# A second layer by Strassen's scheme one pass earlier, with its output weights stored and half of them combined in the first pass

## The chip, the core and the metric

One core of a Trainium2 chip runs the whole kernel. The metric is device time in microseconds (us), from one launch of the program; the time before is the median of three runs. Engines are called by their trace names: PE is TensorE (matmuls; PEld its weight loads), DVE is VectorE, ACT is ScalarE, POOL is GpSimd, SP is SyncE, which here issues all DMA transfers.

## The reference

Decayed linear attention without a softmax, for 8 batches of 8 heads, 576 positions and head size 64, and behind it a feed-forward layer on 4,608 tokens (512 to 2,048 to 512):

```python
scores = scale * np.matmul(q, k.transpose(0, 1, 3, 2))
Dmat = np.where(rel >= 0, gamma[:, None, None] ** rel[None, :, :], 0.0)
attn = np.matmul(scores * Dmat[None, :, :, :], v)
x = attn.transpose(0, 2, 1, 3).reshape(B * S, H * D)
h = x @ w_in
g = np.maximum(h, 0.0) + np.log1p(np.exp(-np.abs(h)))     # softplus
return g @ w_out
```

## The kernel before

Every float32 operand of a matmul is split into a high and a low part of the faster format float32r, and each product is made of three matmuls (low x high, high x low, high x high). All large matmuls are 128 x 128 by 512 columns.

The tokens are nine units of 512. Unit 0 is computed while the weights arrive. The other eight go in four passes of two units: pass 0 has units 1 and 2, pass 1 units 3 and 4, and so on. In a pass the first layer is done by Strassen's scheme on 2 x 2 blocks (seven products in place of eight), over the two units, two halves of the input and a pair of 128-wide pieces of the hidden layer. There are eight such pairs, J = 0 to 7 in the code (NJ = 8). A product takes six matmuls (`product`, line 876 in its loop).

The second layer has two forms:

- Plain: for each piece p of the hidden layer and each 128 tokens, three matmuls into one of four banks y (`output_mm`, line 510). The softplus values of the second unit are sent to DRAM as kept parts and fetched again when that unit's turn comes.
- Full: the softplus values of both units stay on chip in G (the tiles g, placed over the output weights' own tiles, which by then have been stored to DRAM), and the second layer too is done with seven block products (`second`, line 1164). Its weight blocks come from DRAM through the ring: plain ones from outsplit, combined ones (sums S1 to S4 of blocks) from outcombined. Two of the seven are done inside a pair (`full_pair`); five follow as phases over all eight pairs (`full_phase`), the first of which, S4, collects in the PSUM tile named two.

`FULL = 2` says that passes 0 and 1 use the plain form and passes 2 and 3 the full form.

Pass 0 is mixed in its first layer too. While the combined input weights are not all there, pairs 0 to 4 of units 1 and 2 run as ten plain slots each (`plain_slot`: two products, twelve matmuls of the second layer, and in every other slot one attention group). Between those of unit 1 and those of unit 2 the Strassen pairs 5 to 7 run (`strassen_pair`). Then unit 2 finishes from its kept parts. By the trace, unit 1's slots start at about 118 us, pass 1 at 315.15, pass 2 at 500.57 and pass 3 at 676.41.

Attention goes on beside all this: 29 groups of small 64 x 64 matmuls (`chunk_products`), one each in two slots or one pair, each for a chunk of 128 tokens. It computes the scores of one chunk and the values of the one before, into two and third; DVE then masks the scores out of two (L252, tile a), scales the values out of two (L437, tile xs) and updates the states from third (L279, L290). The operands keys and qv are loaded one group ahead, and POOL scales the part v of qv (L187) before the sums of that group use it.

Every engine works through its instructions in the order in which the code issues them. Weight blocks go through a ring of eight tiles; each `product` or `second` requests the block for the eighth one behind it. Combining an output pair j is three steps: `whole_out` (DVE, two sums of high and low, L657), `combine_out` (DVE, four operations on 128x256, L670), and the split into high and low (ACT L674, two casts; DVE L678, two differences), and then two stores of 512 KB to outcombined. Storing it plainly (`store_plain`) is a store of 256 KB and one of 512 KB to outsplit. Before the change this is done in pass 1, pair by pair, and for pair 7 partly in pass 2. In unit 1's slots and the Strassen pairs of pass 0 the input weights are combined by the same operations (`prepare...`), and the combinations of x for the next pass are made by `start...` and `finish...`.

## Time and profile before

| | us |
|---|---|
| median of 3 runs | 830.55 |
| the three runs | 829.44, 830.55, 835.12 |
| the profiled execution, its own time | 834.61 |
| its span from the first to the last instruction | 832.8 |
| PE busy | 822.0 (99%) |
| DVE busy | 516.3 (62%) |
| ACT busy | 377.2 (45%) |
| DMA packets of the data queue | 204.26 MB, 73.7% of 16 engines |

Matmuls overlap, so PE's busy time shows that it is hardly ever without one and not how long a single one takes; for that, a chain of equal matmuls is divided by their number. The views used are the page, the chain in order of time, the waits, the timelines of single engines and the busy time by stretch.

### The profile page before, as it was taken

Reading aid. Unit: us, or ns where it says so; the run is one execution under the profiler, and the core shown is the slowest. Engines: PE = TensorE matmul, PEld = TensorE weight load, DVE = VectorE, ACT = ScalarE, POOL = GpSimd, SP = SyncE. Lnnn points to the kernel's source line nnn. Section 1 sums busy time; section 2 is a strip of 40 time slices with the busy share of each in tenths; the row PEclk is TensorE's granted clock in tenths of the full one; section 3 lists DMA queues with packets and bytes.
Section 4 is the critical chain, followed back from the end, with each engine's and each line's share of the span. In section 5 each row is a group of like instructions: output and inputs, shape, how many; then the busy total and the mean of one; then the engine's idle time right before and its main releaser. Section 6 shows DMA issues by size and latency. Waiting matters only on the chain.

```text
span 832.8 us, 18575 instructions
## 1 busy us (share of the span) xinstructions
PE 822.0 (99%) x7367; PEld 676.3 (81%) x7367; DVE 516.3 (62%) x883; ACT 377.2 (45%) x655; POOL 119.3 (14%) x223
## 2 busy tenths in 40 slices
PE   8999999999999999998999999999999999999998
PEld 6788888888888888887888888888888888888886
DVE  5998967664456686554553753564768953234786
ACT  6888863244332245332432443433345644344553
POOL 4312321221221410111111000211100000000000
PEclk9999999999999999999999999999999999999999
DMA  9998879767778754997989516878856686666674
GB/s 358 313 312 302 297 249 388 247 221 247 252 232 288 250 201 132 352 325 257 311 302 316 195 51 220 273 250 271 277 157 218 197 261 197 193 193 194 196 217 158
DMA packets 138069, 205.44 MB, mean 247 GB/s; under 512 B 10368, under 2 KB 99968, under 8 KB 137984
## 3 DMA queue, kind: packets, MB, share of 16 engines
q1 hardware_dynamic: 137984, 204.26, 73.7%
q8 instruction: 59, 0.97, 0.5%
q14 instruction: 26, 0.21, 0.1%
HBM read 157.56 MB, written 46.66 MB: 245 GB/s over the span
## 4 chain that ended last, share of the span: by engine, by line
PE 94%; DMA 3%; DVE 2%; issue 0%; SPq 0%; ACT 0%; DVEq 0%
PE y L510 27%; PE acc L876 21%; PE two L876 13%; PE sum L1164 12%; PE h L476 5%; PE third L876 3%; PE two L1164 3%; PE third L210 2%; PE two L194 2%; PE two L298 2%; PE two L310 1%; DMA raw<-others 1%; PE third L1164 1%; PE acc L1164 1%; DMA raw<-whole 1%
## 5 line engine op out<-in xcount | busy, mean ns | idle before, releaser
L510 PE MATMUL y<-wout,g 128*128 128x512 f32 x960 | 234.6, 393 | 0.7 <-DVE g L498 0.7
L510 PEld LDWEIGHTS y<-wout,g 128*128 128x128 f32 x960 | 179.3, 189 | 38.9 <-PE h L476 1.1
L876 PE MATMUL acc<-xt,ring 128*128 128x512 f32 x780 | 196.7, 390 | 0.0
L876 PEld LDWEIGHTS acc<-xt,ring 128*128 128x128 f32 x780 | 146.8, 188 | 30.9
L876 PE MATMUL two<-xt,ring 128*128 128x512 f32 x486 | 123.6, 390 | 0.0
L1164 PE MATMUL sum<-parts,ring 128*128 128x512 f32 (+1 forms) x483 | 115.7, 390 | 0.1
L876 PEld LDWEIGHTS two<-xt,ring 128*128 128x128 f32 x486 | 91.1, 188 | 19.4 <-DVE g L1189 0.5
L1164 PEld LDWEIGHTS sum<-parts,ring 128*128 128x128 f32 x483 | 89.7, 188 | 19.2 <-DVE parts L1157 0.5
L1157 DVE TENSOR_TENSOR parts<-g,parts 128x512 fp32r<-128x512 f32 x112 | 75.5, 687 | 40.3 <-ACT parts L1153 37.6
L1153 ACT CAST parts<-g 128x512 fp32r<-128x512 f32 x112 | 69.3, 623 | 47.5 <-PE sum L1164 18.1
L494 ACT CAST g<-ab 128x512 fp32r<-128x512 f32 x58 | 36.0, 621 | 72.5 <-PE y L510 66.9
L187 POOL TENSOR_TENSOR qv<-qv,consts_sb 128x256 f32<-128x256 f32 x61 | 44.6, 732 | 164.4 <-DMA qv<-others 156.8
L498 DVE TENSOR_TENSOR g<-ab,g 128x512 fp32r<-128x512 f32 x58 | 42.6, 735 | 27.1 <-ACT g L494 26.5
L1174 ACT ACTIVATE g<-g 128x512 f32<-128x512 f32 x48 | 30.2, 629 | 42.4 <-DVE g L1189 24.8
L1189 DVE TENSOR_TENSOR g<-two,g 128x512 f32<-128x512 f32 x16 | 11.1, 691 | 61.8 <-PE two L876 59.1
L476 PE MATMUL h<-xt,win 128*128 128x512 f32 x192 | 47.5, 396 | 0.0
L252 DVE TENSOR_TENSOR a<-two,mask 128x512 f32<-128x512 f32 (+1 forms) x28 | 19.0, 678 | 44.5 <-PE third L210 24.7
L476 PEld LDWEIGHTS h<-xt,win 128*128 128x128 f32 x192 | 35.3, 188 | 8.1 <-DVE win L596 0.5
L502 ACT ACTIVATE ab<-quad 128x512 f32<-128x512 f32 x33 | 20.9, 632 | 38.7 <-DVE quad L1008 16.1
L210 PEld LDWEIGHTS third<-qv,keys 64*64 64x64 f32 x776 | 27.1, 134 | 8.9 <-issue 8.1
L210 PE MATMUL third<-qv,keys 64*64 64x64 f32 x776 | 32.8, 222 | 0.1
L194 PE MATMUL two<-qv,keys 64*64 64x64 f32 x880 | 31.5, 221 | 0.0
(173 smaller groups left out, 1123.3 us busy)
## 6 DMA issues: line engine op xcount, KB each, us to landing
ring<-split SPq DMA_DIRECT2D x121, 256.0 KB, 4.2
ring<-combined SPq DMA_DIRECT2D x108, 256.0 KB, 3.9
qv<-others SPq DMA_DIRECT2D x61, 320.0 KB, 5.0
wst<-w SPq DMA_DIRECT2D x32, 512.0 KB, 6.2
ring<-outcombined SPq DMA_DIRECT2D x64, 256.0 KB, 3.4
keys<-others SPq DMA_DIRECT2D x61, 256.0 KB, 5.1
ring<-outsplit SPq DMA_DIRECT2D x48, 256.0 KB, 3.4
split<-win SPq DMA_DIRECT2D x16, 512.0 KB, 6.6
```

What stands on the lines that cost most here:

```text
L187: nc.gpsimd.tensor_mul(v, v, f.unsqueeze(2).broadcast_to([P, 4, D]))
L194: nc.tensor.matmul(L["S"][rows[t], h, part[s]], L["k"][rows[h], s, part[t]], L["q"][rows[h], s, part[t]], start=True, stop=True, skip_grou ...
L210: mm = nc.tensor.matmul(L["T"][rows[h], t, part[s]], L["kp"][rows[t], s, rows[h]], L["v"][rows[t], s, rows[h]], start=True, stop=True, ski ...
L476: nc.tensor.matmul(h, wins[p][:, a, kt * P:(kt + 1) * P], xt[:, b, T1 + half, kt % 2], start=(n == 0), stop=(n == 3 * NKT - 1))
L494: nc.scalar.copy(g[:, HI], ab)
L498: nc.vector.tensor_sub(g[:, LO], ab, g[:, HI].bitcast(F32))
L510: nc.tensor.matmul(ys[u][tt], g[:, a, tt * P:(tt + 1) * P], wouts[p][:, b], start=(p == 0 and n == 0), stop=(p == NF - 1 and n == 2))
L876: nc.tensor.matmul(bank, w[:, ta, kt * P:(kt + 1) * P], xt[:, tb, x, kt], start=start and k == 0, stop=k == 5, skip_group_check=True)
L1153: nc.scalar.copy(t[:, HI], g_slot(J, n))
L1157: nc.vector.tensor_sub(t[:, LO], g_slot(J, n), t[:, HI].bitcast(F32))
L1164: nc.tensor.matmul(bank[m][:, x], w[:, a, m * P:(m + 1) * P], t[:, b, x], start=start and n == 0, stop=n == 2, skip_group_check=True)
L1174: nc.scalar.activation(c, c, AF.Softplus)
```

## The change

`FULL` becomes 1: pass 1 too does its second layer in the full form. G lies over the tiles of the output weights, so these have to be stored before pass 1, and their combinations 4 to 7 have to be read from them before the pair that covers them.

- All eight plain stores move into pass 0: pairs 0 to 4 in unit 1's slots 1, 3, 5, 7, 9, pairs 5 to 7 in unit 2's slots 0, 2, 4 (they are queued and leave with the next products).
- Output pairs 0 to 3 are combined in pass 0: 0 in unit 1's slots 3 to 8, 1 and 2 in Strassen pairs 6 and 7, 3 in unit 2's slots 4 to 8. The preparation of input pairs 7 and 4 moves into Strassen pair 5.
- Output pairs 4 to 7 are combined inside the full pairs of pass 1; the job lists of pass 1 and pass 2 differ from before in that, and in where the combined x is started. The split of block B22 for pass 2 moves into its pair 0.

```diff
-FULL = 2
+FULL = 1
@@ unit 1's slots, (slot, function, arguments)
-        (2, prepare_store, PLAIN), (2, half_b22, 0), (2, start_here, 0), (2, prepare_whole, PLAIN + 1, 0, 1),
-        (3, finish_here, 0), (3, prepare_whole, PLAIN + 1, 1), (4, half_b22, 1), (4, start_here, 1),
...
+        (2, prepare_store, PLAIN), (2, half_b22, 0), (2, start_here, 0), (2, prepare_whole, PLAIN + 1),
+        (3, finish_here, 0), (3, whole_out, 0), (4, half_b22, 1), (4, start_here, 1), (4, prepare_sums, PLAIN + 1),
+        (5, finish_here, 1), (5, prepare_split, PLAIN + 1), (5, combine_out, 0, 0, 2), (5, prepare, PLAIN + 2),
+        (6, prepare_store, PLAIN + 1), (6, half_b22, 2), (6, start_here, 2), (6, combine_out, 0, 2),
+        (7, finish_here, 2), (7, split_out, 0), (7, prepare_ring, PLAIN - 1, 0, 2), (8, store_out, 0),
+        (8, half_b22, 3), (8, start_here, 3), (8, prepare_ring, PLAIN - 1, 2, 4), (9, finish_here, 3),
+        (9, prepare_whole, PLAIN + 2), *[(2 * j + 1, store_plain, j) for j in range(PLAIN)])
@@ Strassen pairs
-    extras = {(FULL - 1, J): J for J in range(NJ - 1)}
-    earlier = {(0, PLAIN): (PLAIN + 2,), (0, PLAIN + 1): (PLAIN - 1,)}
+    extras = {(0, PLAIN + 1): 1, (0, PLAIN + 2): 2}
+    earlier = {(0, PLAIN): (PLAIN + 2, PLAIN - 1)}
@@ unit 2's slots
+            more_jobs = schedule((4, whole_out, 3), (6, combine_out, 3), (7, split_out, 3), (8, store_out, 3),
+                                 *[(2 * n, store_plain, first + n) for n in range(NJ - first)])
@@ full passes
         if s == FULL:
-            last = NJ - 1
-            job(0, lambda: whole_out(last, spare[:2]))
-            job(1, combine_out, last)
-            job(2, lambda: combine_split(raws["out", last]))
-            job(3, queue_store, last)
+            for at, f, *args in ((0, whole_there, 4, 0), (0, whole_there, 5, 2), (1, combine_out, 4), (2, split_out, 4),
+                                 (2, queue_store, 4), (2, combine_out, 5), (3, split_out, 5), (3, queue_store, 5),
+                                 (3, whole_there, 6, 0), (4, combine_out, 6), (4, whole_there, 7, 2),
+                                 (5, split_out, 6), (5, queue_store, 6), (5, combine_out, 7), (6, split_out, 7),
+                                 (6, queue_store, 7), (6, start, 0)):
+                job(at, f, *args)
         if more:
-            for i in range(2):
-                job(4 + i, start, i)
+            if s == FULL:
+                job(divmod(15, NJ), start, 1)
+            else:
+                for i in range(2):
+                    job(4 + i, start, i)
...
-        else:
+        if s > FULL:
             job("x", half_x, B22, STAGE[1, 1], whole, nc.vector)
```

A job with number n of a full pass runs in pair n + 1.

Three places show the order. The first is PE in a pair of pass 1 (attention left out): of before, pair 1 (the numbers behind y and wout are those of the tiles):

```order
L876 MATMUL acc<-xt,ring 128x512 x6
L876 MATMUL two<-xt,ring 128x512 x6
L510 MATMUL y_4274<-wout_179,g 128x512 x3
L510 MATMUL y_4275<-wout_179,g 128x512 x3
L876 MATMUL two<-xt,ring 128x512 x6
L876 MATMUL acc<-xt,ring 128x512 x6
L876 MATMUL two<-xt,ring 128x512 x6
L510 MATMUL y_4276<-wout_179,g 128x512 x3
L510 MATMUL y_4277<-wout_179,g 128x512 x3
L876 MATMUL acc<-xt,ring 128x512 x6
```

and of the change, the same pair (L1167 is what line 1164 was):

```order
L876 MATMUL acc<-xt,ring 128x512 x6
L876 MATMUL two<-xt,ring 128x512 x6
L876 MATMUL acc<-xt,ring 128x512 x6
L876 MATMUL two<-xt,ring 128x512 x6
L876 MATMUL acc<-xt,ring 128x512 x6
L876 MATMUL two<-xt,ring 128x512 x6
L1167 MATMUL sum<-parts,ring 128x512 x6
L876 MATMUL acc<-xt,ring 128x512 x6
L1167 MATMUL sum<-parts,ring 128x512 x6
```

The rows of line 510 are gone from the pair, and two blocks of the full form have come; its other five follow behind pair 7. Over a pass that is 384 matmuls of line 510 against 336.

The second place is DVE at the end of pair 7, the last before the phases. Before (pass 2, which is the first full pass; L1157 splits one G tile into the parts of a second-layer block):

```order
L1251 TENSOR_TENSOR g_7055<-g_7055 128x512
L1252 TENSOR_TENSOR g_7055<-g_7055,g_7054 128x512
L1157 TENSOR_TENSOR parts<-g_5952,parts 128x512
L437 TENSOR_TENSOR xs<-two,consts_sb 128x2x2x128
L1157 TENSOR_TENSOR parts<-g_6164,parts 128x512
```

and of the change (pass 1, now the first full pass; L1254, L1255 and L1160 are the lines that were L1251, L1252 and L1157):

```order
L1254 TENSOR_TENSOR g_5212<-g_5212 128x512
L1255 TENSOR_TENSOR g_5212<-g_5212,g_5211 128x512
L678 TENSOR_TENSOR quad<-quad 128x512 x2
L456 TENSOR_TENSOR quad<-xs 128x256
L457 TENSOR_TENSOR quad<-xs,quad 128x256
L458 TENSOR_TENSOR quad<-xs 128x256
L459 TENSOR_TENSOR quad<-xs,quad 128x256
L1160 TENSOR_TENSOR parts<-g_4110,parts 128x512
L252 TENSOR_TENSOR a<-two,mask 128x512
L437 TENSOR_TENSOR xs<-two,consts_sb 128x2x2x128
L279 TENSOR_TENSOR u<-third,s 128x256
L290 TENSOR_TENSOR s<-third,u 128x256
```

The split of output pair 7 and the start of a combined x now stand ahead of the read-outs of two (L252, L437), and there is a masked read-out, since pass 1's last group has scores.

The third place is SP in unit 1's slots 1 and 2, one piece of the difference (split is the input weights, outsplit the plain output weights):

```order
 L628 DMA ring<-split_112 128x2x256 x2
-L628 DMA ring<-split_113 128x2x256 x2
+L628 DMA ring<-split_113 128x2x256
+L980 DMA outsplit_139<-wout_179 256x1x256
+L628 DMA ring<-split_113 128x2x256
+L982 DMA outsplit_140<-wout_180 128x1024
 L146 DMA keys<-others 128x512
 L152 DMA qv<-others 128x640
```

Two stores of output pair 0 have come in ahead of the operands of an attention group; pairs 1 to 7 follow in the same way.

## Rows read from the trace of the kernel before

**Rows 1.** The page, parts 1 and 4: busy time, and the last chain by engine

```profile
PE 822.0 (99%) x7367; PEld 676.3 (81%) x7367; DVE 516.3 (62%) x883; ACT 377.2 (45%) x655; POOL 119.3 (14%) x223
PE 94%; DMA 3%; DVE 2%; issue 0%; SPq 0%; ACT 0%; DVEq 0%
```

**Rows 2.** Waits of PE: us in total, times, longest us

```profile
PE two L310 <- issue: 2.3, 1, 2.3
```

**Rows 3.** The chain in order of time: start us, us, what

```profile
144.87 2.72 PE acc L876 x12
...
238.61 2.72 PE acc L876 x12
...
347.98 1.59 PE y L510 x6
...
365.18 1.59 PE y L510 x6
...
382.27 2.31 issue
...
403.82 1.59 PE y L510 x6
...
508.91 5.44 PE y L510 x24
...
590.26 1.59 PE sum L1164 x6
...
620.28 9.52 PE two L1164 x42
```

**Rows 4.** The page, part 5: busy us and mean ns of line 510's matmuls

```profile
L510 PE MATMUL y<-wout,g 128*128 128x512 f32 x960 | 234.6, 393 | 0.7 <-DVE g L498 0.7
```

**Rows 5.** One stretch: length, busy us (instructions) by engine, PEclk, DMA share, GB/s

```profile
385.00:388.50 3.50, 3.50 (x10) 2.73 (x10) 2.04 (x4) 0.59 (x1) 1.40 (x3) 0.51 0.70 258
```

**Rows 6.** DMA from 382 to 383.2 us: packets, MB, share of 16 engines

```profile
q8 instruction: 1, 0.02, 4.6%
```

**Rows 7.** Passes 1 and 2, line 510 alone: length, PE, PEld, PEclk, DMA

```profile
315.15:500.57 185.42, 94.53 (x385) 72.18 (x384) 0.99 0.73 252
500.57:676.41 175.84, 5.60 (x24) 4.50 (x24) 1.00 0.74 236
```

**Rows 8.** Pass 2, line 1164 alone, same columns

```profile
500.57:676.41 175.84, 80.00 (x336) 62.36 (x336) 1.00 0.74 236
```

**Rows 9.** Timeline of DVE, pairs 3 and 5 of pass 2: start us, us, what

```profile
559.11 1.28 DVE L678 TENSOR_TENSOR quad<-quad 128x512 fp32r<-128x512 f32 x2
...
588.09 0.42 DVE L456 TENSOR_TENSOR quad<-xs 128x256 f32<-128x256 f32 x1
...
589.22 0.42 DVE L459 TENSOR_TENSOR quad<-xs,quad 128x256 f32<-128x256 f32 x1
590.31 0.69 DVE L252 TENSOR_TENSOR a<-two,mask 128x512 f32<-128x512 f32 x1 [0.67 <-PE third L210]
590.92 0.68 DVE L437 TENSOR_TENSOR xs<-two,consts_sb 128x512 f32<-128x512 f32 x1
```

**Rows 10.** Three stretches, columns as in rows 5

```profile
118.00:142.00 24.00, 23.93 (x245) 19.61 (x244) 14.62 (x28) 9.41 (x16) 5.54 (x12) 1.00 1.02 356
142.00:304.00 162.00, 162.00 (x1935) 134.34 (x1934) 97.16 (x177) 54.22 (x92) 39.40 (x69) 1.00 0.77 258
...
334.00:455.00 121.00, 118.69 (x1272) 98.12 (x1272) 59.72 (x105) 43.92 (x74) 16.74 (x35) 0.99 0.90 309
```

**Rows 11.** Timeline of POOL, the second scaling of v of a group

```profile
145.61 0.77 POOL L187 TENSOR_TENSOR qv<-qv,consts_sb 128x256 f32<-128x256 f32 x1 [0.85 <-DMA qv<-others]
...
238.05 0.62 POOL L187 TENSOR_TENSOR qv<-qv,consts_sb 128x256 f32<-128x256 f32 x1 [0.88 <-DMA qv<-others]
```

**Rows 12.** Timeline of SP, the stores of unit 2's slot 8

```profile
289.07 1.03 SPq L686 DMA_DIRECT2D combined<-quad  x2
```

**Rows 13.** Timeline of ACT, the first read of kept part 5

```profile
301.59 0.62 ACT L494 CAST g<-quad 128x512 fp32r<-128x512 f32 x1 [1.10 <-PE y L510]
```

More of the change, by code (lines that the diff above doesn't have):

```diff
@@ L657, in whole_out, with combine_out @@
             nc.vector.tensor_add(a[:, HI], w[:, HI].bitcast(F32), w[:, LO].bitcast(F32))
-    def combine_out(j):
+    def combine_out(j, first=0, upto=4):
         f = raws["out", j]
@@ L662, in combine_out @@
         (a11, a21), (a12, a22) = ((a[:, 0], a[:, 1]) for a in blocks[0])
-        combine_blocks(a11, a12, a21, a22, blocks[1], nc.vector)
+        combine_blocks(a11, a12, a21, a22, blocks[1], nc.vector, first, upto)
     def combine_blocks(a11, a12, a21, a22, sums, engine, first=0, upto=4):
@@ L1012, in strassen_pair @@
             whole_out(extra)
-        for j in early:
-            if j > PLAIN:
-                prepare_whole(j)
-            else:
-                prepare_sums(j, 0, 2)
+        for j in early[:1]:
+            prepare_sums(j)
         if last:
@@ L1023, in strassen_pair @@
         nc.scalar.copy(c[1], z)
-        for j in early:
-            prepare_sums(j, 0 if j > PLAIN else 2)
+        for j in early[1:]:
+            prepare_sums(j)
         if extra is not None:
@@ L1056, in strassen_pair @@
         if extra is not None:
-            combine_store(outs_dram[extra], raws.pop(("out", extra)))
+            store_out(extra)
         if group:
@@ L1108, in retention_softplus_ffn @@
                 (8, finish_combined, 0, nc.vector), (9, finish_combined, 1, nc.vector))
+            more_jobs = schedule((4, whole_out, 3), (6, combine_out, 3), (7, split_out, 3), (8, store_out, 3),
+                                 *[(2 * n, store_plain, first + n) for n in range(NJ - first)])
+            plan = {p: plan.get(p, []) + more_jobs.get(p, []) for p in range(2 * first)}
             starts = schedule((6, start_combined, 0), (8, start_combined, 1, nc.vector),
@@ L1134, in retention_softplus_ffn @@
                 f()
-            if s == FULL - 1 and J == NJ - 1:
-                store_plain(J)
             kept_parts(u2, J, kept[n], 1)
@@ L1318, in start, with whole_there @@
     def start(i):
-        tmps[i] = spare[(2, 3, 4, 2)[i]].rearrange("p n (a b c) -> p (n a) b c", a=2, b=2)
+        tmps[i] = spare[(4, 3, 2, 4)[i]].rearrange("p n (a b c) -> p (n a) b c", a=2, b=2)
         combined_x([tmps[i][:, n] for n in range(4)], column(i), nc.vector)
+    def whole_there(j, at):
+        whole_out(j, spare[at:at + 2])
     def lead(a, b):
```

19 lines of the change are left out of this document (8 added, 11 removed).

## The prediction

> **What bounds the kernel now.** I read the page first. TensorE is busy 99% of the span and makes 94% of the chain that ended last; VectorE has 62%, ScalarE 45% [rows 1]. The waits of TensorE come next: the longest in the whole span is 2.3 us, and it is put down to "issue", to nothing that the profile shows [rows 2]. From 142 to 304 us it was busy for 162.00 of 162.00 us [rows 10]. So time is the number of matmuls times their step, plus what a new wait adds, and any work that stays behind TensorE is free. Then the chain in order of time gives the step. 42 matmuls of the second layer take 9.52 us and 24 of the plain form 5.44 us [rows 3]: 226.7 ns each for both forms. The 393 ns that the page prints as the mean of one [rows 4] overlaps its neighbours and is no price.
>
> The profiled execution took 834.61 us (span 832.8) and the median run 830.55. The difference is one event in pass 1. Pairs there take 17.20 us (347.98 to 365.18), but the two that begin at 365.18 end at 403.82, 38.64 us, 4.24 more than two pairs should [rows 3]. In it TensorE stood still for 2.31 us at 382.27 inside an attention group, and the granted clock was 0.51 of full speed, about its 1.2 GHz level, right behind (385 to 388.5) [rows 3, 5]; before it TensorE had been busy without a gap. One 16 KB block of the instruction queue moved just there [rows 6]. 834.61 - 4.24 = 830.4 is the median run, so I take that event out of the base: 830.4.
>
> **What is removed and added on TensorE.** In pass 1 (315.15 to 500.57) line 510 has 384 matmuls of the plain second layer (the row counts one at the edge); pass 2 (500.57 to 676.41) has 336 of line 1164, and 24 of line 510 left over from pass 1 [rows 7, 8]. After the change pass 1 is built like pass 2: -384 + 336 = -48 matmuls, 48 x 226.7 = 10.9 us. First-layer products and attention keep their number. The windows agree: pass 1 without its event is 185.42 - 4.24 = 181.2 us, pass 2 is 175.84, so pass 1 becomes 5.3 shorter, and pass 2 loses its 24 left-over matmuls, 5.4. Sum **-10.7 to -10.9**; I take -10.9, the count. Here a page differs from the rows. The Trainium skill (TensorE: Matmul & The Clock Gate, Back-to-back issue gap) puts sustained matmuls of 512 columns at about 131 ns. By it the saving would be an estimated 6.3 us and the time 4.6 longer than mine; no stretch of this trace steps at that rate.
>
> **VectorE in pass 1.** Four pairs of output weights (4 to 7) are now summed, combined and split inside the full pairs 1 to 7, where pass 2 before had one. The place that can hurt is the end of a pair: the attention results a and xs are read out of the PSUM tile two, which a later product overwrites. In pair 5 of pass 2, VectorE is free for jobs at 588.09 and the group's last matmul ends as the next sum begins, 590.26: 2.17 us of cover [rows 3, 9]. Two L678 cost 1.3, the four of L456 to L459 1.5 (588.09 to 589.64), and four L670 are of the same shape, 1.5; two L657 are like two L678, 1.3 [rows 9]. In pairs 1 to 6 the jobs are at most 2.8 us, so the read-outs begin up to 0.6 late and need 0.6 + 0.7 = 1.3 more. The next write of two lies a sum (1.59) and a product (1.36) behind, 2.95. Covered, 1.0 to spare: **0**; if that cover were gone, 0.5 to 1 us in each of six pairs.
>
> Pair 7 is different. There the order shows six jobs (2.8 us) and one more split (0.6) ahead of L252: 3.4 - 2.17 = 1.2 late, read-outs done 2.5 after the group. And no product follows: the first S4 block writes two directly behind the sum, 1.6 after the group. **+0.9 us.** Before, the pass that ended this way had no jobs in pair 7 and no masked scores to read (its last group has values only). Bounds: 0, if the splits run closer than I add them, and 1.5 if the two states that follow also hold up the next split. Behind it the phases get one more start of the combined x, 1.5 us, at a place where four split buffers let VectorE run ahead; 0. ScalarE gets two casts a pair beside 45%; 0. The S4 block of pair 7 is loaded from the store that has just left; the load is issued behind the second S4 block and has six blocks, 8 us, to wait for the store and land: 0, at worst 2 us.
>
> **The DMA queue in pass 0.** Eight stores of 768 KB (6.3 MB) and four of 1 MB move ahead of 316 us, 10.5 MB; 142 to 304 us has share 0.77 at 258 GB/s [rows 10]. That is 31 us of transfers into 37 us of free DMA time: the share goes to about 0.96. Pass 1 ran with 0.90 from 334 to 455, and of the 121.00 us TensorE missed 2.31 there, all of it the event above [rows 10]. Weight blocks are requested eight ahead, which is four plain slots, so they stand delays. The attention operands don't: they are requested when the group before has ended, and POOL scales v before the sums use it. I looked where a moved store stands right ahead of such loads on SP and how early POOL was:
> - Slot 4 of unit 1: stores of pair 0 (768 KB) now precede the loads. DMA was full there (1.02, 356 GB/s), so +2.2 us. POOL ended at 146.38, the group starts at 144.87 + 2.72 = 147.59 [rows 3, 11]: 1.2 of cover, **1.0 late**.
> - Slot 1 of unit 2: the 1 MB of outcombined 2 goes out just ahead, 2.9 us. POOL ended at 238.67, the group starts at 241.33 [rows 3, 11]: **0.2 late**.
> - The other groups have more cover than 2.2 us by the same reading, if the queue has drained by then: 0.
> Sum +1.2; bounds 0 (the free 0.23 takes the stores) and 4 (two more groups 1.4 late). In pass 1 the stores that moved are gone, 8.4 MB of kept parts (written and read) go too, and 14.7 MB of ring blocks come, evenly spaced as in pass 2: 0. The fetch of kept part 5 now waits for a store of slot 8 to land; before, those stores left SP at 289.07 and part 5 was first read at 301.59 [rows 12, 13], 12.5 us for a store and a fetch: 0, at worst 1.
>
> **Sum** against the profiled execution: 834.6 - 4.2 - 10.9 + 0.9 + 1.2 = **821.6 us**, 1.1% below the median run. About 1% is what a measurement of this kernel can tell from no change, and this lies on that edge.
>
> **Rivals.**
> (B) The event at 382 us comes back in most runs. For it: a DMA queue at 0.96, and in pass 1 the block boundaries of TensorE's instructions fall elsewhere in the groups. Against it: one of 28 groups had it, and from 118 to 142 us, at share 1.02, TensorE was busy 23.93 of 24.00 us [rows 10]. Price 4.2: 825.8. The Trainium skill speaks against it (Runtime: NRT & Kernel Launch, Instruction fetch mechanics): an engine fetches its instructions in 16 KB blocks by its own DMA, at a cost that is mostly hidden. By that B would have hardly a chance; the 2.3 us at 382.27 are the one place of this trace that it doesn't fit.
> (C) Every cover holds: 834.6 - 4.2 - 10.9 = 819.5. For it: pass 1 hid seven such weight pairs and the same stores. Against it: pair 7, counted above.
> (D) The other side: the first pass becomes DMA-bound. If the queue never drains from 118 to 304 us, attention operands fall behind by 31 us less the free time that they can really use. It decides from 10.9 us uncovered, about a third of 31, on; with half uncovered (15.5) the kernel takes 819.5 + 15.5 = 835.0, slower. For it: the share of 1.02 at 118 to 142. Against it: 37 us are free, and even behind that stretch the operands came 1.2 us early.
> (E) Matmuls step otherwise than now (131 ns): -6.3 in place of -10.9, 826.2. Both forms step alike in the rows, so this has next to no chance.
>
> **How the numbers follow.** Forecast, stalls of 1 to 4 us: 0.50. B 0.22, C 0.14, D 0.12 (half of it slower than 830.55), E 0.02. The likeliest gives 821.6, its own range 820 to 824. From C less 0.9 (the runs shown lie 1.1 below their median) to B plus 1.7 for the upper DMA bound, 818.6 to 827.5 holds some 0.8. Faster by over 1% means under 822.2: C and about three quarters of the forecast's half, 0.51. Slower by over 1%, above 838.9, is the far end of D: 0.06. Within 1%: 0.43.
>
> **What would show it.** In the profile of the changed kernel: line 510 with 576 matmuls and the second layer with 336 more; pass 1 near 176 us; in pair 7 of pass 1 a wait of TensorE for the read-out of xs of about 0.9 us; a wait for POOL's scaling of 1 us in slot 4 of unit 1; DMA share above 0.9 from 142 to 304 us. Wrong: an idle of some us with the clock at its lower level (B); several waits for qv or POOL in a row before 300 us (D); no wait at all (C).

## The result, and the profile after

The changed kernel takes **822.80 us** (median of six runs, 822.05 to 825.55) against 830.12 for the kernel before, measured beside it (six runs, 829.44 to 835.12). The ratio is 0.9907, with a 95% interval from 0.988 to 0.9933: 0.9% faster. The forecast was 821.6, with a range of 818.6 to 827.5. The profiled execution took 822.85 us, with a span of 821.1 us.

The page, parts 1, 4 and 5 (the lines that answer to [rows 1, 4]):

```profile
PE 809.5 (99%) x7319; PEld 665.5 (81%) x7319; DVE 559.0 (68%) x953; ACT 388.1 (47%) x681; POOL 123.8 (15%) x223
...
PE 87%; DVE 6%; DMA 4%; issue 1%; ACT 1%; SPq 0%; POOL 0%; DVEq 0%; ACTq 0%; POOLq 0%
...
L510 PE MATMUL y<-wout,g 128*128 128x512 f32 x576 | 140.1, 392 | 0.7 <-DVE g L498 0.7
```

7367 matmuls have become 7319, 48 fewer, and line 510 has 576 of them where it had 960. The second line is the one to stop at: VectorE's part of the chain that ended last went from 2% to 6%, and TensorE's from 94% to 87%. TensorE is as busy as it was, but for 34 us (445.65 to 479.96) the chain now runs through VectorE and ScalarE (experiment 2).

The second layer by pass, line 1167 (it was 1164) alone, from the first product of pass 1 to that of pass 2, and so on to pass 3 (columns: stretch and length, PE and PEld busy with instructions, PEclk, DMA share, GB/s):

```profile
316.39:494.83 178.44, 80.08 (x336) 62.28 (x336) 1.00 0.78 252
494.83:664.98 170.15, 80.00 (x337) 62.36 (x336) 1.00 0.73 228
```

Against [rows 7, 8], pass 1 went from 185.42 to 178.44 us and has the same 336 matmuls of this form as pass 2 (the row of pass 2 counts one more at its edge). Pass 2 lost its 24 left-over matmuls, 175.84 to 170.15. The granted clock is 1.00 in both: nothing like the event at 382 us is in this execution.

Waits of TensorE, the view of [rows 2] (us in total, times, longest us):

```profile
PE two L1167 <- ACT parts L1156: 1.1, 1, 1.1
PE third L210 <- POOL qv L187: 0.7, 1, 0.7
...
PE two L876 <- DVE quad L1015: 0.6, 1, 0.6
PE two L194 <- DMA keys<-others: 0.6, 1, 0.6
```

These four are new and single, one place each. From start to start of the matmuls around them they cost 1.26 us (437 us, end of pair 7 of pass 1), 0.72 (242, slot 1 of unit 2), 0.76 (186, Strassen pair 5) and 0.55 (346, pair 1 of pass 1). Two small ones, 0.28 at 479 and 0.17 at 228, bring the sum to 3.7 us.

First pass and pass 1 by stretch (columns as in [rows 5]):

```profile
118.00:142.00 24.00, 23.93 (x245) 19.59 (x244) 15.27 (x29) 9.24 (x16) 4.99 (x12) 1.00 1.03 370
142.00:304.00 162.00, 160.66 (x1926) 132.43 (x1925) 112.05 (x206) 57.58 (x100) 39.74 (x67) 1.00 0.90 313
```

Against [rows 10], the DMA share from 142 to 304 us rose from 0.77 to 0.90, not to 0.96, and TensorE missed 1.3 us of the 162.

### The profile page after: what moved, and what is told of

Same layout as the page of the kernel before. It is cut to its first block, busy times and chain, and to the rows that moved or that the text cites. A ratio compares the mean times of both kernels' runs of the same rounds, so it can differ in the third digit from the quotient of the medians.

```text
span 821.1 us, 18673 instructions
## 1 busy us (share of the span) xinstructions
PE 809.5 (99%) x7319; PEld 665.5 (81%) x7319; DVE 559.0 (68%) x953; ACT 388.1 (47%) x681; POOL 123.8 (15%) x223
## 4 chain that ended last, share of the span: by engine, by line
PE 87%; DVE 6%; DMA 4%; issue 1%; ACT 1%; SPq 0%; POOL 0%; DVEq 0%; ACTq 0%; POOLq 0%
PE acc L876 21%; PE sum L1167 16%; PE y L510 16%; PE two L876 13%; PE h L476 5%; PE two L1167 4%; PE third L876 3%; DVE parts L1160 2%; PE third L210 2%; PE two L194 2%; PE two L298 2%; PE two L310 1%; PE third L1167 1%; PE acc L1167 1%; DMA raw<-others 1%; DMA raw<-whole 1%
## 5 line engine op out<-in xcount | busy, mean ns | idle before, releaser
L1167 PE MATMUL sum<-parts,ring 128*128 128x512 f32 (+1 forms) x723 | 174.3, 391 | 0.2
L1167 PEld LDWEIGHTS sum<-parts,ring 128*128 128x128 f32 x723 | 134.0, 188 | 29.2 <-DVE parts L1160 1.0
L1160 DVE TENSOR_TENSOR parts<-g,parts 128x512 fp32r<-128x512 f32 x168 | 114.4, 697 | 54.2 <-ACT parts L1156 53.3
L510 PE MATMUL y<-wout,g 128*128 128x512 f32 x576 | 140.1, 392 | 0.7 <-DVE g L498 0.7
L1156 ACT CAST parts<-g 128x512 fp32r<-128x512 f32 x168 | 104.0, 622 | 69.9 <-PE sum L1167 26.2
L510 PEld LDWEIGHTS y<-wout,g 128*128 128x128 f32 x576 | 107.1, 188 | 23.7 <-PE h L476 1.1
L1177 ACT ACTIVATE g<-g 128x512 f32<-128x512 f32 x72 | 45.3, 629 | 60.6 <-DVE g L1192 35.6
L1192 DVE TENSOR_TENSOR g<-two,g 128x512 f32<-128x512 f32 x24 | 16.6, 692 | 76.2 <-PE two L876 76.2
L1190 ACT COPY g<-acc 128x512 f32<-128x512 f32 x24 | 14.1, 588 | 78.4 <-PE acc L876 78.4
L1227 ACT ACTIVATE g<-acc 128x512 f32<-128x512 f32 x24 | 14.3, 598 | 49.1 <-PE acc L876 49.1
L1167 PE MATMUL two<-parts,ring 128*128 128x512 f32 x144 | 33.7, 390 | 1.1 <-ACT parts L1156 1.1
L252 DVE TENSOR_TENSOR a<-two,mask 128x512 f32<-128x512 f32 (+1 forms) x28 | 19.0, 677 | 21.8 <-PE third L210 15.0
```

The costliest lines, as they stand in the source:

```text
L252: nc.vector.tensor_mul(a[:, :, at], src.rearrange("p h (s c) -> p h s c", c=HC), mask.unsqueeze(1).unsqueeze(1).broadcast_to([P, 2, 2 * le ...
L510: nc.tensor.matmul(ys[u][tt], g[:, a, tt * P:(tt + 1) * P], wouts[p][:, b], start=(p == 0 and n == 0), stop=(p == NF - 1 and n == 2))
L1156: nc.scalar.copy(t[:, HI], g_slot(J, n))
L1160: nc.vector.tensor_sub(t[:, LO], g_slot(J, n), t[:, HI].bitcast(F32))
L1167: nc.tensor.matmul(bank[m][:, x], w[:, a, m * P:(m + 1) * P], t[:, b, x], start=start and n == 0, stop=n == 2, skip_group_check=True)
L1177: nc.scalar.activation(c, c, AF.Softplus)
```

## The experiments

The lowest run of the kernel before is 829.44, 829.80, 829.54 and 829.64 us in the four sets of runs, so the sets agree to some 0.4 us where this kernel runs undisturbed. Its median doesn't: it lies at 830.12, 832.57, 831.61 and 831.09, for a reason that experiment 1 looks for. The changed kernel was measured in the first set alone, and the runs of one kernel lie 0.8 to 5.3 us apart. So differences of under 1 us between medians are not clear of noise, and the ratios, each against the median of its own set, can't be compared with each other; where small differences are given below, it is the profiles that carry the reading. A "wait" in us below is the start-to-start distance of two matmuls, less the 0.23 us of an undisturbed step.

| kernel | median us (lowest to highest, runs) | ratio to before, 95% |
|---|---|---|
| changed kernel | 822.80 (822.05 to 825.55, 6) | 0.9907 (0.988 to 0.9933) |
| moves alone | 834.79 (831.98 to 837.28, 10) | 1.0023 (0.9996 to 1.0049) |
| before, shifted | 830.27 (829.75 to 831.09, 10) | 0.9979 (0.9964 to 0.9993) |
| moves alone, shifted | 832.38 (831.54 to 833.41, 10) | 1.0007 (0.999 to 1.0023) |
| start 0 later | 823.48 (822.81 to 825.32, 4) | 0.9876 (0.9831 to 0.9921) |
| whole weights earlier | 822.13 (821.64 to 823.38, 4) | 0.9859 (0.9815 to 0.9903) |
| stores behind loads | 822.13 (821.06 to 822.96, 4) | 0.9856 (0.9811 to 0.99) |
| rows behind keys | 822.38 (822.17 to 823.02, 4) | 0.9888 (0.9863 to 0.9914) |
| 4.2 MB more stores | 823.03 (822.35 to 823.81, 4) | 0.9898 (0.9867 to 0.9929) |
| 8.4 MB more stores | 826.18 (824.55 to 828.91, 7) | 0.9927 (0.9901 to 0.9952) |
| all four edits | 820.44 (820.27 to 821.90, 4) | 0.9868 (0.9841 to 0.9894) |
| starts in gaps | 819.54 (819.05 to 819.81, 4) | 0.984 (0.9807 to 0.9873) |

### 1. The moves without the matmuls, and the event at 382 us

```diff
-FULL = 1
+FULL = 2
```

> The changed kernel with FULL = 2: the stores and combinations of output weights stand in the first pass as in the changed kernel, but the second pass keeps its plain second layer, so all 48 matmuls are back. If the gain is the matmul count (48 x 226.7 ns = 10.9 us) less the stalls of the move, this kernel is slower than the kernel before by those stalls: the three waits that the changed kernel's trace has before 300 us are 0.76 (185.8 us), 0.17 (227.9) and 0.72 (241.9), and the wait at the end of pair 7, now one pass later, is up to 1.3; so 1.6 to 3.0 us above before, 831.7 to 833.1 if before reads 830.1. If moving the stores is itself what gained (transfers spread more evenly), it is at or below before: 826 to 830. If the matmuls step at 131 ns, taking them away is worth 6.3 and this kernel lies 6.3, not about 10, above the changed one.

Measured: 834.79 us, nine of ten runs above 834, one at 831.98. That is above what either theory gave, and the waits of before 300 us don't explain it. The waits of TensorE in this kernel show why:

```profile
PE third L210 <- issue: 1.5, 1, 1.5
PE two L1167 <- ACT parts L1156: 0.9, 1, 0.9
PE third L210 <- POOL qv L187: 0.7, 1, 0.7
...
PE two L876 <- DVE quad L1015: 0.6, 1, 0.6
```

The last three are the changed kernel's, as expected (the first of them one pass later). The first is the event of [rows 2, 3] again: put down to "issue", in the same attention group, that of pair 3 of pass 1, at 383.92 us. This kernel issues the same matmuls as the kernel before up to there, but not the same transfers. From 383 to 385 us the data queue was far from full (parts 3 of the view of DMA: queue, packets, MB, share of 16 engines):

```profile
q1 hardware_dynamic: 301, 0.35, 56.1%
q8 instruction: 1, 0.02, 3.1%
```

So a full queue isn't needed for it. What the two kernels share is TensorE's stream of instructions, and the stalls stand at the same point of it: counted over each trace, 8,385 of TensorE's recorded instructions (matmuls, weight loads and semaphore instructions) begin before the stall, in the kernel before as in this one. Two more kernels shift that stream and change nothing else: the kernel before and the kernel with the moves alone, each with 16 tiny matmuls in the opening (32 matmul instructions and their weight loads, 64 in all):

```diff
     for n in range(OPENING):
         nc.tensor.matmul(idle[:, 0, 0:2 * C], fill[:, 0:P], fill[:, 0:2 * C], start=True, stop=True)
+    for n in range(16):
+        nc.tensor.matmul(idle[0:32, 0, 0:32], fill[:, 0:32], fill[:, 0:32], start=True, stop=True)
```

> The kernel before with 16 tiny matmuls (32 x 32, nobody reads them) put into the opening, so that TensorE's whole stream of instructions lies 64 instructions later and every block of 16 KB begins elsewhere in the attention groups. They cost up to 3 us at the start, less what TensorE waits there for its first operands (about 1 us). Of 29 runs of the kernel before, 13 lay above 832, up to 837, the others at 829.4 to 832. If the event at 382 us belongs to where a block of instructions begins inside that group, it is gone or elsewhere: the runs lie within 1.5 us of each other (in one of two kernels moved like this, about; a new place can be as bad), and the profile shows no wait of over 1 us put down to issue in that group. If it belongs to what else moves at that time (stores, operands), the same spread of 7 us stays, and the wait stays in that group.

> The kernel with the moves alone (FULL = 2), shifted in the same way. Unshifted it had runs from 831.98 to 837.28, nine of ten above 834, and its profile has a wait of 1.5 us put down to issue in the same attention group of the second pass (383.9 us) as the kernel before. If the position of the blocks makes it, the runs come together at 832 to 833 plus the 1 to 3 us of the tiny matmuls, less spread than 2 us; then the moves alone cost 1.6 to 3.0 us, as expected of that run. If not, the spread stays.

(The count in the first of these is 12 of 29, not 13.) Measured: the kernel before, shifted, has ten runs from 829.75 to 831.09. Unshifted, 18 of its 48 runs in all sets lie above 832 us. The moves alone, shifted: ten runs from 831.54 to 833.41, median 832.38, where nine of ten unshifted were above 834. In neither profile does TensorE wait over 0.3 us for "issue". The tiny matmuls themselves cost nothing visible: in the shifted kernel before, TensorE begins its first products of loaded operands at 8.69 us; unshifted, it begins half of them at 7.33, waits for the operands of the rest and goes on at 8.67.

What follows: the runs point to where TensorE stands in its own stream of instructions, and not to the stores or operands that move then. The times alone are not proof. Beside the shifted kernel before, 6 of 19 unshifted runs lay above 832, so ten runs without one would come by chance in some 20 to 40 sets once; and the moves alone, unshifted, were measured in another set, on another chip. The position is the stronger sign: both stalls behind 8,385 instructions, and in the shifted kernel before the one wait for "issue" that is left (0.27 us at 584.64) behind 12,481, which is 4,096 = 16 x 256 further.

That blocks of instructions arriving late are the cause is the likeliest reading, no more: a block of 16 KB did move there [rows 6], and the 59 blocks, if all are TensorE's, make 256 to a block for its 15,114 recorded instructions, while the 128 small matmuls of an attention group and their weight loads are 256 instructions issued within 1.9 us. A group thus uses up a whole block in the time of eight big matmuls. Which step of the fetch comes late, no run shows, nor why this group is hit and others with a boundary are not. The Trainium skill (Runtime: NRT & Kernel Launch, Instruction fetch mechanics) calls the cost of a block's boundary mostly hidden. The shifted kernels agree, with no wait for "issue" over 0.3 us; if the stall of 2.3 us at 382 us is such a boundary, it is an exception. Of the 18 runs above 832 us none was profiled; 12 of the 17 whose clock is on record have a mean of 0.996 to 0.998, like the profiled execution (0.998), but that all of them have this stall is not shown.

And they give the clean price of the moves: 832.38 - 830.27 = **2.1 us** slower with no matmul removed, inside the 1.6 to 3.0 that was expected. (The profile of the moves alone, shifted, has 0.77 us at Strassen pair 5, 0.15 at 228 and 1.02 at the end of pair 7; the wait at slot 1 of unit 2 is not in it.) The gain is the 48 matmuls. The best kernel below (819.54), which has no new wait over 0.25 us, and the shifted kernel before (830.27), measured beside it, lie **10.7 us** apart: 48 x 226.7 ns is 10.9.

### 2. Pair 7 of pass 1: who is late there, and who is late next

In the changed kernel, VectorE at the end of pair 7 (timeline: start us, us, engine, line, operation):

```profile
433.72 1.29 DVE L678 TENSOR_TENSOR quad<-quad 128x512 fp32r<-128x512 f32 x2
434.93 0.42 DVE L456 TENSOR_TENSOR quad<-xs 128x256 f32<-128x256 f32 x1
...
436.26 0.41 DVE L459 TENSOR_TENSOR quad<-xs,quad 128x256 f32<-128x256 f32 x1
436.60 0.68 DVE L1160 TENSOR_TENSOR parts<-g,parts 128x512 fp32r<-128x512 f32 x1
437.20 0.68 DVE L252 TENSOR_TENSOR a<-two,mask 128x512 f32<-128x512 f32 x1
437.80 0.68 DVE L437 TENSOR_TENSOR xs<-two,consts_sb 128x512 f32<-128x512 f32 x1
```

And TensorE there:

```profile
435.82 1.66 PE L1167 MATMUL sum<-parts,ring 128*128 128x512 f32 x6
438.58 1.60 PE L1167 MATMUL two<-parts,ring 128*128 128x512 f32 x6 [1.10 <-ACT parts L1156]
```

The view of waits names ScalarE's cast. But the write of `two` at 438.58 comes 0.10 us after the read-out of xs by L437 ends (437.80 + 0.68), and the cast (437.52 + 0.63 = 438.15 in the chain) had been done for 0.43. So the reading is that VectorE released it. The edit takes 1.5 us of VectorE's work from ahead of it:

```diff
-                                 (6, queue_store, 7), (6, start, 0)):
+                                 (6, queue_store, 7), (divmod(11, NJ), start, 0)):
```

> The changed kernel with start 0 (the four operations that make the first combined x, 1.5 us of VectorE) moved from pair 7 of the second pass into phase block (1, 3), behind the read-outs of the PSUM tile two. If the wait of 1.26 us at 437 us is VectorE's backlog ahead of the read-outs, it goes, and nothing comes in its place: 1.1 to 1.3 us faster than the changed kernel, 821.6 if that reads 822.8. If TensorE waits there for ScalarE's cast (line 1156, to which the view of waits puts it down), the wait stays: same time within 0.3 us. The third possibility: the four operations hold up a split in the phase, and a new wait of up to 1.5 us appears near 450 us.

Measured: 823.48 us, 0.7 above the changed kernel's median and not the 1.1 to 1.3 below it of the first theory. TensorE:

```profile
435.32 1.66 PE L1167 MATMUL sum<-parts,ring 128*128 128x512 f32 x6
436.82 3.56 PE L1167 MATMUL two<-parts,ring 128*128 128x512 f32 x15
...
479.60 2.58 PE L1167 MATMUL sum<-parts,ring 128*128 128x512 f32 x10 [1.17 <-DVE parts L1160]
```

The wait at the end of pair 7 is gone: `two` follows the sum after 1.50 us instead of 2.76. The profiles of the five other kernels that keep start 0 in that pair have it, at 1.26 to 1.30 us. So VectorE it was. But 42 us later stands a wait of 1.33 us in place of the 0.28 that the changed kernel has there. It is the third possibility, at 478 us instead of 450. Busy time by stretch shows the reason. The first row is the phases of pass 1 in the changed kernel, the second the same stretch of its pass 2, which starts one combined x less there:

```profile
444.00:484.00 40.00, 39.88 (x177) 32.69 (x176) 37.95 (x63) 24.10 (x38) 1.38 (x2) 1.00 0.73 220
614.40:654.40 40.00, 39.94 (x177) 32.72 (x176) 35.85 (x58) 24.23 (x39) 0.00 (x0) 1.00 0.69 207
```

VectorE (third busy time) is busy for 37.95 of 40 us, against 35.85 where nothing waits over 0.25 us. The sum alone doesn't decide it. The kernel of this experiment has no more from 444 to 484 us, but the wait of 1.33; and pass 2 of the changed kernel has nearly as much in a stretch that lies 3.6 us later in the pass, and no wait over 0.25 us:

```profile
444.00:484.00 40.00, 38.75 (x170) 31.31 (x169) 37.97 (x64) 23.31 (x38) 0.89 (x2) 1.00 0.75 227
618.00:658.00 40.00, 39.94 (x177) 32.72 (x176) 37.85 (x61) 25.18 (x41) 0.00 (x0) 1.00 0.72 216
```

What counts is the work that lies ahead of the wait. In the 32 us up to it VectorE has 30.87 in this kernel, 30.65 in the changed kernel, and 29.64 in the same 32 us of pass 2; in this kernel its gaps of over 0.1 us there are 0.16 and 0.76 us, both before 469. The chain of the changed kernel runs through it: from 445.65 to 479.96 us its pieces are VectorE's and ScalarE's, and end with

```profile
477.99 0.61 DVE quad L1278
478.60 0.02 issue
478.62 0.69 DVE c L1279
479.31 0.61 DVE parts L1160
479.92 0.04 issue
479.96 2.11 PE sum L1167 x8
```

Work that is put into the phases thus comes out at their end. The other place for the starts is inside the pairs: VectorE waits there 1.7 us on either side of the addition into c11 (L1192). Starts 0 and 1 go behind it, in pairs 6 and 7, together with the three edits of the next section:

```diff
         for f in jobs.pop("x", []):
             f()
+        if s == FULL and J >= NJ - 2:
+            start(J - NJ + 2)
...
-        tmps[i] = spare[(4, 3, 2, 4)[i]].rearrange("p n (a b c) -> p (n a) b c", a=2, b=2)
+        tmps[i] = spare[(4, 1, 2, 4)[i]].rearrange("p n (a b c) -> p (n a) b c", a=2, b=2)
...
-                                 (6, queue_store, 7), (6, start, 0)):
+                                 (6, queue_store, 7)):
                 job(at, f, *args)
         if more:
-            if s == FULL:
-                job(divmod(15, NJ), start, 1)
-            else:
+            if s > FULL:
```

> As the kernel with all four edits, but starts 0 and 1 stand where VectorE waits for a product (behind the addition into c11 of pairs 6 and 7, with 1.7 us idle on each side), instead of in the phases, where VectorE is busy for 37.95 of 40 us. If VectorE is the bound of the phases from 444 to 484 us, 3 us less work there take away the wait of 1.56 us at 476 us, and it is 1.0 to 1.4 faster than the kernel with four edits: 819.0 to 819.5 if that reads 820.4. If the wait at 476 us is the read-out of the sums (lines 1278 and 1279) whatever ran before, it stays, and the time is the same within 0.3. If the starts hold up the pairs, a wait appears at 412 or 427 us.

Measured: **819.54 us**, 0.90 below the kernel with four edits (820.44), a little under the 1.0 to 1.4 expected. TensorE runs on from 471.73 us with no wait over 0.25 us, and in the same stretch of the pass VectorE has what pass 2 has, 35.86 us of 40:

```profile
471.73 8.47 PE L1167 MATMUL sum<-parts,ring 128*128 128x512 f32 x35
```

```profile
439.50:479.50 40.00, 39.94 (x176) 32.74 (x176) 35.86 (x58) 24.00 (x38) 1.66 (x2) 1.00 0.74 232
```

VectorE was the bound at the end of the phases; with the starts out of them the wait is gone. This version is faster than both kernels: ratio 0.984 (0.9807 to 0.9873) to the kernel before.

### 3. The three other waits

Each edit is held against the profiles of the other kernels that lack it: a wait that is missing there too is not shown to have gone by the edit.

**Strassen pair 5 (185.8 us).** VectorE and TensorE in the changed kernel:

```profile
184.47 1.70 DVE L642 TENSOR_TENSOR quad<-quad 128x512 f32<-128x512 f32 x2
186.09 0.68 DVE L1015 TENSOR_TENSOR quad<-two,quad 128x512 f32<-128x512 f32 x1
```

```profile
186.82 1.66 PE L876 MATMUL two<-xt,ring 128*128 128x512 f32 x6 [0.60 <-DVE quad L1015]
```

The addition that frees `two` stands behind whole weights of pair 7, which the change put into slot 9 of unit 1. The edit moves these one slot up:

```diff
-        (8, half_b22, 3), (8, start_here, 3), (8, prepare_ring, PLAIN - 1, 2, 4), (9, finish_here, 3),
-        (9, prepare_whole, PLAIN + 2), *[(2 * j + 1, store_plain, j) for j in range(PLAIN)])
+        (8, half_b22, 3), (8, start_here, 3), (8, prepare_ring, PLAIN - 1, 2, 4),
+        (8, prepare_whole, PLAIN + 2), (9, finish_here, 3), *[(2 * j + 1, store_plain, j) for j in range(PLAIN)])
```

> The changed kernel with prepare_whole(7) (two additions on line 642, 1.70 us of VectorE) in slot 8 of unit 1, where VectorE has 1.55 us idle, instead of slot 9. If the wait of 0.76 us at 185.8 us is this work ahead of the addition into c0 (line 1015), it goes: 0.7 to 0.8 us faster than the changed kernel, 822.0 if that reads 822.8. If finish_here 3 in the same slot (1.7 us) is enough to make VectorE late, 0.2 to 0.5 stays. If the work is merely passed on, the wait appears again in slot 9 (near 182 us).

Measured: 822.13 us, 0.67 less; no wait for L1015 is left in its profile, and none in slot 9. The eight profiles without this edit all have the wait, at 0.63 to 0.80 us. The first theory holds.

**Slot 1 of unit 2 (241.9 us).** The issuing queue, POOL and TensorE in the changed kernel:

```profile
231.27 2.43 SPq L686 DMA_DIRECT2D outcombined<-quad  x2
233.80 0.73 SPq L146 DMA_DIRECT2D keys<-others  x1
...
236.38 0.43 SPq L152 DMA_DIRECT2D qv<-others  x1
```

```profile
242.14 0.68 POOL L187 TENSOR_TENSOR qv<-qv,consts_sb 128x256 f32<-128x256 f32 x1 [0.86 <-DMA qv<-others]
```

```profile
241.69 0.27 PE L210 MATMUL third<-qv,keys 64*64 64x64 f32 x1
...
242.88 0.27 PE L210 MATMUL third<-qv,keys 64*64 64x64 f32 x1 [0.73 <-POOL qv L187]
```

The edit puts `store_out(extra)` behind the attention group and its loads in `strassen_pair`:

```diff
-        if extra is not None:
-            store_out(extra)
         if group:
             ...
+        if extra is not None:
+            store_out(extra)
```

> The changed kernel with the stores of combined output weights (1 MB each, pairs 6 and 7 of the first pass) issued behind the loads of the attention operands instead of ahead of them. If the wait of 0.72 us for POOL's scaling of v at 241.9 us is the 2.43 us that the store takes on the issuing queue and the 3 us that its bytes take on the wires, the loads leave 2.4 us earlier and the wait goes: 0.7 us faster than the changed kernel, 822.1 if that reads 822.8. If the operands are late because all 16 engines are full from 230 to 240 us whatever the order, the wait stays at 0.4 to 0.7.

Measured: 822.13 us, 0.67 less, and the wait is gone; the last load of qv left at 233.48 us instead of 236.38. Of the eight profiles without this edit seven have the wait, at 0.42 to 0.79 us, and one (moves alone, shifted) has none. So the order on the queue made it, with a margin that is not always used up.

**Pair 1 of pass 1 (346.3 us).** Four stores of output rows leave ahead of the operands of the next group:

```profile
332.18 3.15 SPq L543 DMA_DIRECT2D out<-quad  x4
335.43 0.62 SPq L146 DMA_DIRECT2D keys<-others  x1
...
339.60 0.59 SPq L146 DMA_DIRECT2D keys<-others  x1
```

```diff
-        queued_some(len(queued))
+        held = queued[:] if s == FULL and J == 0 else []
+        queued_some(len(queued) if not held else 0)
+        del queued[:]
         if group:
             ...
+        queued.extend(held)
```

> The changed kernel with the four stores of output rows at the end of pair 0 of the second pass (3.15 us on the issuing queue) queued behind the attention loads of the next group instead of ahead of them. If the wait of 0.55 us for keys at 346.25 us comes from these stores, which make the loads leave 2.1 us later than in the kernel before, it goes: 0.5 us faster than the changed kernel, 822.3 if that reads 822.8. If the second load of keys is late because it leaves fourth, one for each weight product, the wait stays. The stores now hold two buffers longer: if the additions of whole weights in pair 1 need these, a new wait of VectorE appears there, and up to 1 us is lost.

Measured: 822.38 us, 0.42 less, and no wait for keys. The second load left at 338.37, 1.2 us earlier. That the edit did it is not shown: three profiles with the old order (whole weights earlier, stores behind loads, 4.2 MB more stores) have no wait there either, and in the first two the second load left at 338.09 and 338.26 us behind the same four stores. In the other two it is 0.19 (start 0 later) and 1.08 us (8.4 MB more). The wait varies from one execution to the next; that the four stores add to it was argued and not shown.

**All four together** (start 0 later and these three):

> The changed kernel with all four edits: start 0 later, whole weights of pair 7 a slot earlier, stores of combined weights behind the attention loads, output rows behind the keys. The four waits are 1.26 + 0.76 + 0.72 + 0.55 = 3.29 us. If they are independent and each edit takes its own away, 819.5 us where the changed kernel reads 822.8 and the kernel before 830.1: that is rival C of the prediction, every cover holds, 48 x 226.7 ns = 10.9 below before. If removing one lets the next come up (what waits is passed on), 820.5 to 822.

Measured: 820.44 us, 2.36 less of the 3.29. The three waits of this section are not in its profile; the fourth has moved to 475.6 us (1.33 us), as in experiment 2.

### 4. How much the first pass can still transfer

Spare stores of 512 KB of output weights, which nobody reads, with each pair of stores that the change moved into the first pass:

```diff
+    spared = [dram.tile([P, 2, PIECE], F32R, name=f"spared{n}") for n in range(8)]
     def store_plain(j):
+        for t in spared[1 * j:1 * j + 1]:
+            queued.append(lambda t=t: nc.sync.dma_start(t.bitcast(F32), wouts[2 * j + 1].bitcast(F32)))
```

> The changed kernel with eight more stores of 512 KB of output weights in the first pass (4.2 MB that nobody reads), one with each pair of stores that the change moved there. The share of the DMA engines from 142 to 304 us is 0.90, that is 16 us of free time; 4.2 MB at the 313 GB/s of that stretch are 13.4 us. If transfers are hidden as long as free time is left (the prediction), the share rises to 0.97 or 0.98 and the time by 0 to 1.5 us, from operands that come later behind single stores. If the first pass is already bound by its transfers (rival D), the time rises by about as much as the transfers take, 8 to 13 us.

> The same with two spare stores of 512 KB each time, 8.4 MB: 27 us of transfers into 16 us of free time. The prediction's view: beyond the free time the rest shows, 11 us at most, less what spills behind 304 us, where the share is 0.34 to 0.75 (up to 8 us of room by 330 us); so 3 to 11 us above the changed kernel, with waits for qv or keys in several groups in a row. If the engines' share is no measure of what they can still take, either nothing happens (0 to 1.5 us) or the 4.2 MB already cost as much in proportion.

Measured: 823.03 with 4.2 MB, 826.18 with 8.4 MB, that is +0.2 and +3.4 us. From 142 to 304 us, with 4.2 and then with 8.4 MB:

```profile
142.00:304.00 162.00, 160.94 (x1926) 132.77 (x1925) 111.34 (x206) 57.94 (x100) 39.59 (x67) 1.00 0.96 340
```

```profile
142.00:304.00 162.00, 158.78 (x1913) 130.65 (x1912) 111.58 (x204) 56.10 (x98) 36.78 (x67) 1.00 0.98 358
```

With 4.2 MB TensorE loses nothing more, as expected. With 8.4 MB operands are late in several groups, and the time lies at the lower end of the expected 3 to 11 us. The share doesn't tell the two apart where it happens. From 230 to 304 us, again with 4.2 and then with 8.4 MB:

```profile
230.00:304.00 74.00, 73.54 (x1001) 60.84 (x1000) 49.92 (x95) 22.09 (x37) 20.01 (x36) 1.00 0.95 339
230.00:304.00 74.00, 71.47 (x990) 58.96 (x989) 49.75 (x93) 20.12 (x36) 18.65 (x36) 1.00 0.95 344
```

The second kernel comes out of a fuller stretch (142 to 190 us: share 1.04 against 1.00), and its operands are later behind it; the largest waits that the first lacks are 1.5 us at 285 and 1.1 at 350, in pass 1. One of these waits shows how a late operand spreads on POOL, which works in order:

```profile
282.80 0.68 POOL L187 TENSOR_TENSOR qv<-qv,consts_sb 128x256 f32<-128x256 f32 x1 [0.89 <-DMA qv<-others]
283.44 0.91 POOL L456 TENSOR_TENSOR quad<-xs 128x256 f32<-128x256 f32 x1
...
286.89 0.09 POOL L348 MEMSET mark<- 1x1 f32 x1
```

The scaling waits for qv, the four operations of a combined x stand behind it, and the mark of 0.09 us for which TensorE waits in the group stands behind these: 1.5 us lost there. So added transfers do come to cost something, between 4.2 and 8.4 MB more than the change moved. Rival D in full is not reached even then: the second 4.2 MB, 13.4 us of transfers, cost 3.2 us by the medians, and two of the seven runs behind this median have a lower mean clock (0.997 and 0.998).

## Why the prediction was right, and where it was not

- **-10.9 for 48 matmuls: right.** 10.7 us between two kernels without new waits (experiment 1). The chain of the changed kernel has 42 matmuls of the second layer in 9.52 us again (609.00), 226.7 ns each. By the 131 ns of the Trainium skill (TensorE: Matmul & The Clock Gate, Back-to-back issue gap), rival E, it would have been an estimated 6.3: the measurement decides against it here.
- **-4.24 for the event: right as a base, and in part by luck.** It took the event out because the median of three runs was without it. In later sets 17 of 42 runs lay above 832 us, and there the median of before is up to 832.6; against that set the same base would have been 2 us too low. Rival B got 0.22 for "the event comes back in most runs". It didn't: one of six runs, 825.55 at a mean clock of 0.997, may be one. What the prediction could not tell is that the event seems to hang on the position in TensorE's stream, so that an edit of TensorE's program can move it, for better or worse.
- **+0.9 at the end of pair 7 of pass 1: right in place and cause, 1.26 measured.** The term was mis-sized by small parts of both its sides: the jobs and the split ahead of L252 took 3.48 us (433.72 to 437.20) and not 3.4, the cover was 2.10 (433.72 to the sum's begin at 435.82) and not 2.17, TensorE went on 0.10 after the read-out, and the sum it could fill in took 1.50 and not 1.6. The view of waits put it down to ScalarE; the experiment gave it to VectorE.
- **The starts in the phases at 0, "four split buffers let VectorE run ahead": wrong.** VectorE is at 35.85 of 40 us there in pass 2; one start more and the backlog of pair 7 made it 37.95, with a wait of 0.28 us at the end, and a second start made that wait 1.33. The prediction counted the split buffers and not what VectorE already has to do in the stretch.
- **+1.2 for the DMA queue in pass 0: 0.72 measured, at slot 1 of unit 2, and wrong in both its parts.** Slot 4 of unit 1, priced at 1.0, had no wait: the second scaling ended at 146.85 and the group began at 146.75, but its first matmuls don't need the second v (at slot 1 the group ran for 0.24 us before it stopped for it). Slot 1 of unit 2, priced at 0.2, cost 0.72: POOL had 2.66 us of cover before [rows 3, 11] and ended 1.13 after the group's begin, 3.8 us later and not 2.9. The prediction priced the store's bytes and not its time on the issuing queue: the last load of qv left 3.3 us later than before (236.38 against 233.08), and the store's issue is 2.43 of that. That the term came near its size is luck.
- **Not seen: 0.76 at Strassen pair 5 and 0.55 at pair 1 of pass 1.** The prediction looked at VectorE's backlog only at the ends of the full pairs, and left the work of VectorE that moved into the plain slots at nothing without naming its cover. In slot 9 that work stands ahead of an addition that frees a PSUM tile. In pass 1 it looked at the weight blocks and not at the stores of output rows, which had left in ones and twos before and now leave in a row of four ahead of the keys (a cause that experiment 3 doesn't show).
- **DMA share 0.96 from 142 to 304 us: it was 0.90.** 55 GB/s more over 162 us are 8.9 MB for 0.13 of the time, 21 us; the prediction priced 10.5 MB at 31 us, the rate of the mean. The added transfers took less of the engines per byte than the mean transfer there. That is why rival D was further off than it looked.

The sum: 834.61 - 4.24 - 10.88 + 3.74 = 823.2, measured 822.85 in the profiled execution. Stalls of 3.7 against 2.1 more than make up the 1.2 us by which 821.6 was too low; the likeliest case's own range, 820 to 824 with stalls of 1 to 4 us, held it. Of the 3.7 only 2.0 stand at places that the prediction had priced, and 1.8 at places that it had at 0. Pass 1 was to be near 176 us and took 178.44; without its three waits (1.26, 0.55 and 0.28) it is 176.35.

## What to carry to other kernels

When a change takes matmuls out of a TensorE-bound stretch, count what each other engine has to do in the same stretch afterwards, not its free gaps before, and look where its gaps lie: here a job moved to a place behind which VectorE had hardly a gap left (30.65 of 32 us) was paid at the stretch's end, and the same job in a gap of 1.7 us cost nothing. Look for what is queued, in order, ahead of every read-out that frees a PSUM tile and every load that an attention-like group needs; here three of the four new waits were such an order, and two of them went away by a change of order alone. Look for a wait in several profiles before an edit gets the credit for its going. And compare a kernel with another only over enough runs to see whether one of them has an event that may hang on the position of its instructions: with 16 idle matmuls in the opening ten runs of the kernel before lay within 1.3 us, where 19 measured beside them lay within 5.0.

## What the runs showed of the hardware

- A stall of TensorE with no wait that the profile can name: 2.3 and 1.5 us in two profiles, behind the same 8,385 recorded instructions, in the first with the granted clock at 0.51, its 1.2 GHz level, behind it [rows 5] and in the other without. It also came with the 16 engines at 56%. 18 of 48 runs of one kernel lay above 832 us, and none of ten above 831.1 once its stream lay 64 instructions later.
- The DMA engines moved 358 GB/s on the mean over 162 us (share 0.98) and up to 370 over 24 us. At 0.96 over these 162 us TensorE lost nothing more, at 0.98 it lost 1.9 us more; within them, at the same 0.95 from 230 to 304 us, one kernel lost 0.5 us and the other 2.5, so the share alone doesn't tell whether operands come in time.
- Two stores of 512 KB took 2.43 us of the issuing queue ahead of an attention group's loads and 0.89 us behind them; the last of these loads left at 236.38 us in the one order and at 233.48 in the other.
- The profile named ScalarE for a wait that ended 0.43 us after ScalarE's cast and 0.10 us after VectorE's read-out, and moving VectorE's work took the wait away: compare the distances in time before you take the name.
